# Attention decode with a gated feed-forward: wider runs for two weight matrices, keys three pairs ahead, a word-wise turn

## The chip, the cores and the metric

One core of a Trainium2 chip runs the whole kernel. The metric is the device time of one execution in microseconds (us); for the kernel before it is the median of three runs.

## The reference, cut to what matters

```
# B=8, D=512, Hq=32, Hkv=8, rep=4, Sk=4096, Dh=128, F=1792, all bfloat16
xn = layernorm(x)                                   # (8, 1, 512)
q  = (xn @ wq).reshape(8, 1, 32, 128)
W  = min(4096, max(256, Sk // 4))                   # 1024: only the last 1024 keys count
k, v = k_cache[:, :, Sk-W:], v_cache[:, :, Sk-W:]   # repeated for the 4 query heads of a key head
p  = softmax(q . k * Dh**-0.5)
s  = (p . v).reshape(8, 1, 4096) @ wo
g  = silu((gelu(xn @ w_gate) * (xn @ w_up)) @ w_down)
out = x + s * g                                     # (8, 1, 512)
```

One token of eight sequences. Each weight and each key and value of the window is used once for few rows, so some 47 MB are read for little arithmetic.

## The kernel before, in words

**Loads.** All large loads are issued by SyncE (SP) on one DMA queue, in program order, into a ring of nine buffers of 16 KB a partition (2 MB; pool `big`). A load waits until the work on the tile that had its buffer is done. The order is: `wq` in three DMAs (1, 1 and 2 MB), gate and up matrix, K0, K1, down matrix, V0, K2, V1, K3 and so on to K7, V6, V7, and then `wo`. K0 is the "key pair" of key head 0: one tile with the window of all eight sequences, 128 partitions by two *sets* by 32 keys of 128 elements. A partition holds 32 consecutive keys of one sequence, 8 KB in a run of memory. Set s = 2h + y has the four sequences of parity y. `load_pair` (L102) loads a pair in one DMA, or in two halves, one for each set; only V7 goes in halves. The list `pending` (L537) with `fetch` (L543) gives the order.

**Ahead of the keys.** Layer norm, the queries (L296, 32 matmuls, as `wq` lands), gate and up matmuls (L344), the queries transposed into `qT`, and the masks (`masks`, L239, on VectorE (DVE)).

**The main loop** (L560) runs over half steps t; s, i = divmod(t, 2). In step t a set s gets two of its four transposed quarters (`transpose_quarter`, L422): TensorE (PE) transposes four blocks of 128 x 128 words, two bfloat16 in one FP32 word (L425), and VectorE (L436) or ScalarE (ACT, L438) copies them out of PSUM to `kT`. One set behind follow the scores (L447, eight matmuls on four groups of 32 columns, the even and odd elements of the words), the mask with the row maximum (L455), and the maximum over each query's partitions (`maxima`, L466 and L471). Two sets behind follow the exponentials (L480, with the row sum), a copy of the row sum on GpSimd (POOL, L484), and `turn` (L490), which transposes 32 x 32 blocks of the probabilities. From step `LV` = 7 on, `value_half` (L496) multiplies with the values (L501, 16 matmuls a set in two halves). A value matmul takes a pair of keys at once, so its result has 2 x 128 columns of which one half belongs to each row; both go to `blk` (L508). `gather` (L512) sums each head's rows with eight FP32 matmuls (L518), which pick the right half, divides by the sum (L523, L525) and turns the result (L530) into `oR`, the left operand of the output projection. TensorE works in this written order: a matmul that waits for a load holds back all behind it.

**The feed-forward** hides in it: `hidden_steps` (L359), two in each step; `down` in steps 7 and 8, `fold` and `gate` in step 9.

**The end.** The output matrix comes in seven pieces; row 4p + r of each 512-row block of a head is at partition p, so the four rows of a partition are 4 KB in a run. Pieces are two of 1 MB (two heads each), three of 512 KB, and the last head as 384 and 128 KB. 128 matmuls (L605) sum them, two VectorE operations (L616, L617) apply gate and residual, and ScalarE issues the store (L618).

## Time and profile before

| | |
|---|---|
| median of 3 runs | 120.78 us (120.72 to 120.94) |
| the profiled execution, its own time | 120.92 us |
| its span | 119.1 us |
| granted TensorE clock, mean | 0.971 |
| PE busy | 83.4 us (70%), 974 matmuls |
| DVE / ACT / POOL busy | 64.2 / 56.2 / 5.5 us |
| DMA | 47.60 MB, 6557 packets, mean 400 GB/s |

The span is the profiled part of the execution, from its first to its last instruction; some 1.8 us of the execution lie outside it. Engine shares are averages over stages with different limits; a wait is worth what it moves at the end. "PEld" is TensorE's weight load. The chain that ended last is followed back from the last instruction, and names at each step what released it.

### The profile page before, as it was taken

Reading aid. Unit: us, or ns where it says so; the run is one execution under the profiler, and the core shown is the slowest. Engines: PE = TensorE matmul, PEld = TensorE weight load, DVE = VectorE, ACT = ScalarE, POOL = GpSimd, SP = SyncE. Lnnn points to the kernel's source line nnn. Section 1 sums busy time; section 2 is a strip of 40 time slices with the busy share of each in tenths; the row PEclk is TensorE's granted clock in tenths of the full one; section 3 lists DMA queues with packets and bytes.
Section 4 is the critical chain, followed back from the end, with each engine's and each line's share of the span. In section 5 each row is a group of like instructions: output and inputs, shape, how many; then the busy total and the mean of one; then the engine's idle time right before and its main releaser. Section 6 shows DMA issues by size and latency. Waiting matters only on the chain.

```text
span 119.1 us, 2381 instructions
## 1 busy us (share of the span) xinstructions
PE 83.4 (70%) x974; PEld 57.7 (48%) x974; DVE 64.2 (54%) x172; ACT 56.2 (47%) x94; POOL 5.5 (5%) x25
## 2 busy tenths in 40 slices
PE   0250629519956493979996898399999589966880
PEld 0110216119743353547764666356767348724660
DVE  1400131812799881848775577077787454854330
ACT  4100030204961881675795395249578634673200
POOL 7000000000000000000000000000000000000000
PEclk9999999999999999999999999769999976999999
DMA  3999999999999999999999999999999999999930
GB/s 96 424 451 435 425 424 415 432 421 432 437 420 418 435 424 435 421 416 435 421 432 418 435 424 421 427 427 427 424 440 416 424 429 427 424 409 421 414 136 3
DMA packets 6557, 47.60 MB, mean 400 GB/s; under 512 B 524, under 2 KB 660, under 8 KB 1684
## 3 DMA queue, kind: packets, MB, share of 16 engines
q1 hardware_dynamic: 6496, 47.45, 94.9%
q8 instruction: 7, 0.11, 0.3%
q10 hardware_dynamic: 52, 0.02, 0.1%
q14 instruction: 2, 0.02, 0.0%
HBM read 47.46 MB, written 0.01 MB: 399 GB/s over the span
## 4 chain that ended last, share of the span: by engine, by line
DMA 71%; PE 15%; ACT 5%; DVE 3%; SPq 2%; issue 1%; ACTq 0%
DMA big<-in_A_k_cache_dram 71%; PE kT_ps L425 7%; PE m_ps L518 2%; PE s L605 2%; PE o_ps L501 2%; ACT kT L438 2%; ACT p L480 1%; PE sc L447 1%; ACT L365 1%; SPq L145 1%; SPq L96 1%; PE m_ps L466 1%; DVE pT L490 1%; ACT blk L508 1%; ACT z L365 0%
## 5 line engine op out<-in xcount | busy, mean ns | idle before, releaser
L425 PE MATMUL kT_ps<-identf,big 128*128 128x128 f32 x256 | 39.7, 302 | 9.9 <-DMA big<-in_A_k_cache_dram 9.8
L438 ACT ACTIVATE kT<-kT_ps 128x1024 bf16<-128x1024 bf16 x32 | 32.5, 1021 | 28.7 <-PE kT_ps L425 28.5
L425 PEld LDWEIGHTS kT_ps<-identf,big 128*128 128x128 f32 x256 | 31.5, 154 | 18.2 <-DMA big<-in_A_k_cache_dram 9.9
L436 DVE COPY kT<-kT_ps 128x1024 bf16<-128x1024 bf16 x32 | 22.0, 688 | 19.5 <-PE kT_ps L425 19.3
L480 ACT ACTIVATE p<-sc_sb,bias 128x512 bf16<-128x512 f32 x16 | 11.5, 718 | 6.3 <-DVE bias L471 5.8
L501 PE MATMUL o_ps<-big,pT 128*32 128x256 bf16 x256 | 12.6, 283 | 0.5 <-ACT blk L508 0.5
L490 DVE STREAM_TRANSPOSE pT<-p 128x512 bf16<-128x512 bf16 x16 | 11.3, 705 | 2.3 <-ACT p L480 2.2
L466 PE MATMUL m_ps<-identf,top 128*128 128x128 f32 x32 | 7.4, 311 | 7.0 <-DVE top L455 5.6
L455 DVE CUSTOM_DVE_ANT_0 sc_sb<-sc,own 128x512 f32<-128x512 f32 x16 | 10.5, 659 | 0.7 <-PE sc L447 0.7
L447 PE MATMUL sc<-kT,zeros 128*32 128x512 bf16 x128 | 10.8, 415 | 0.1
L466 PEld LDWEIGHTS m_ps<-identf,top 128*128 128x128 f32 x32 | 4.9, 194 | 9.4 <-DVE top L455 6.7
L518 PE MATMUL m_ps<-blk,sums 128*128 128x129 f32 x64 | 9.0, 281 | 0.4 <-ACT blk L508 0.4
L501 PEld LDWEIGHTS <-pT 128*32 128x32 bf16 x256 | 5.5, 97 | 6.1 <-issue 1.8
L518 PEld LDWEIGHTS m_ps<-blk,sums 128*128 128x128 f32 x64 | 7.9, 191 | 1.0 <-ACT blk L508 0.6
L484 POOL COPY blk<-blk 128x1 f32<-128x1 f32 x16 | 2.9, 184 | 103.7 <-ACT p L480 99.4
L508 ACT ACTIVATE blk<-o_ps 128x256 f32<-128x256 f32 x16 | 6.1, 382 | 2.8 <-PE o_ps L501 2.8
L296 PE MATMUL sc<-big,zeros 128*32 128x512 bf16 x16 | 2.5, 610 | 6.1 <-DMA big<-in_A_wq_dram 6.1
L303 DVE CAST q_row<-sc 128x512 bf16<-128x512 f32 x2 | 1.3, 686 | 9.3 <-PE sc L296 9.3
L471 DVE CUSTOM_DVE_ANT_0 scr<-m_ps,same 128x128 f32<-128x128 f32 x16 | 4.6, 289 | 2.4 <-PE m_ps L466 2.4
L307 ACT ACTIVATE q_row<-o_ps 128x512 bf16<-128x512 f32 x2 | 1.1, 594 | 9.5 <-PE o_ps L296 9.5
L296 PEld LDWEIGHTS <-zeros 128*32 128x32 bf16 x32 | 1.2, 119 | 8.1 <-issue 7.6
L330 DVE COPY zeros<-kT_ps 64x128 bf16<-64x128 bf16 x4 | 1.1, 282 | 4.8 <-PE kT_ps L318 4.1
(68 smaller groups left out, 52.3 us busy)
## 6 DMA issues: line engine op xcount, KB each, us to landing
big<-in_A_k_cache_dram SPq DMA_DIRECT2D x8, 2048.0 KB, 32.2
big<-in_A_v_cache_dram SPq DMA_DIRECT2D x7, 2048.0 KB, 33.7
big<-in_A_wq_dram SPq DMA_DIRECT2D x2, 1024.0 KB, 5.8
big<-in_A_wq_dram SPq DMA_DIRECT2D x1, 2048.0 KB, 11.2
big<-in_A_v_cache_dram SPq DMA_DIRECT2D x2, 1024.0 KB, 30.0
big<-in_A_wo_dram SPq DMA_DIRECT2D x2, 1024.0 KB, 28.0
big<-in_B_w_gate_dram SPq DMA_DIRECT2D x1, 1792.0 KB, 15.0
big<-in_B_w_up_dram SPq DMA_DIRECT2D x1, 1792.0 KB, 18.6
```

The costliest lines, as they stand in the source:

```text
L425: nc.tensor.transpose(ps[:, c, :], K[s][:, 2 * (i * QP + c) : 2 * (i * QP + c) + 2, :] .rearrange("p c d -> p (c d)").bitcast(FP32), identf,)
L436: nc.vector.tensor_copy(out=out, in_=in_)
L438: nc.scalar.activation(out=out, in_=in_, func=ACT.Copy)
L447: nc.tensor.matmul(ps[32 * R : 32 * R + 32], qT[:, e, s].rearrange("p c b j -> p (c b j)"), t[:, :, 32 * R : 32 * R + 32, e], start=(e == ...
L455: nc.vector.tensor_tensor_reduce(out=sc[s], in0=ps.rearrange("p c k -> p (c k)"), in1=own.rearrange("p c b g -> p (c b g)"), op0=ALU.add, ...
L466: nc.tensor.matmul(ps, top.pop(s).to_broadcast([P, P]), identf, start=True, stop=True)
L471: nc.vector.tensor_tensor_reduce(out=scr, in0=ps, in1=same.rearrange("p x n -> p (x n)"), op0=ALU.add, op1=ALU.min, scale=-scale, scalar=- ...
L480: nc.scalar.activation(out=P_[s], in_=sc.pop(s), func=ACT.Exp, scale=scale, bias=biases.pop(s), accum_out=blk[s][:, 0, Dh : Dh + 1],)
L490: nc.vector.transpose(out=pT[s].rearrange("p c k -> p (c k)"), in_=P_.pop(s))
L501: nc.tensor.matmul(o_ps[s][32 * q : 32 * q + 32].rearrange("p c d -> p (c d)"), pT[s][:, c, :], V[s][:, 2 * c : 2 * c + 2, :].rearrange("p ...
L508: nc.scalar.activation(out=blk[s][:, :, 0:Dh], in_=o_ps.pop(s), func=ACT.Copy)
L518: nc.tensor.matmul(ps, sums[:, c, b].rearrange("p j b f -> p (j b f)"), t[:, c, :], start=(b == 0 and c == 0), stop=(b == NB - 1 and c == 1),)
```

## The change

- `wo` is read with eight rows (8 KB) a partition, over blocks of two heads: `oR` and `gather` work on pairs of heads (`x = h % 2` goes to partitions 0 to 63 or 64 to 127 of one PSUM tile). Pieces are three of 1 MB, then 512, 384 and 128 KB.
- The two halves of a value result are joined ahead of the gather: ScalarE scales one by `half[:, 0]`, VectorE adds the other times `half[:, 1]`. `blk` has 129 columns in place of 258, a head has four gather matmuls with 64 output rows in place of eight with 128, and the copy of the row sum is gone.
- The first two k-rows of `wq` come in one DMA of 2 MB (16 KB a partition).
- Keys come three pairs ahead of the values in place of two. K0 and K7 come in halves. Values start at step 9, `down` runs in steps 8 and 9, `fold` and `gate` in step 10; `gather` runs one step later.
- `turn` transposes words of two probabilities. So the score columns are put in the order (pair of chunks, key, which of two), in the score matmul's operand and the mask, and a value matmul's weights have a step of two.
- Masks but for the reductions, two small copies and one memset go from VectorE to GpSimd, one copy to ScalarE.

```diff
-    m_top, m_out = m_ps[:, 0:P], m_ps[:, P : P + Dh + 1]
+    m_top = m_ps[:, 0:P]
+    m_out = m_ps[:, P : P + 2 * (Dh + 1)].rearrange("p (a d) -> p a d", a=2)
...
-    HB = 2 * SET // (rep * D)
+    R8 = 2 * rep
...
     def load_wo(h, r0, n, nh=1):
...
+        t = wo_at(h)[:, h % 2 : h % 2 + nh, r0 * D : (r0 + n) * D]
+        src = A_wo.rearrange("(h p k) n -> p h (k n)", p=P, k=R8)
+        src = src[:, h : h + nh, r0 * D : (r0 + n) * D]
+        if nh == 1:
+            nc.sync.dma_start(out=t[:, 0, :], in_=src[:, 0, :])
...
-    for k0, cuts in ((0, (1, 1)), (2, (2,))):
+    for k0, cuts in ((0, (2,)), (2, (2,))):
...
-        nc.vector.tensor_copy(out=xf, in_=ps)
+        nc.scalar.activation(out=xf, in_=ps, func=ACT.Copy)
...
-    own = consts.tile([P, CP, 32 // G, G], FP32, name="own")
+    own = consts.tile([P, CP // 2, 32 // G, G, 2], FP32, name="own")
...
-    sums = consts.tile([P, 2, 2, rep, B, PB], FP32, name="sums")
+    sums = consts.tile([P, NB, 2, rep // 2, B, PB], FP32, name="sums")
...
-    oR = rows.tile([P, Hkv, rep, 32], BF16, name="oR")
+    oR = rows.tile([P, Hkv // 2, 2 * rep, 32], BF16, name="oR")
...
-                    t[:, :, 32 * R : 32 * R + 32, e],
+                    t.rearrange("p (c a) k e -> p c k a e", a=2)[
+                        :, :, 32 * R : 32 * R + 32, :, e
+                    ],
...
-        nc.gpsimd.tensor_copy(
-            out=blk[s][:, 1, Dh : Dh + 1], in_=blk[s][:, 0, Dh : Dh + 1]
-        )
...
     def turn(s):
-        pT[s] = p_pool.tile([P, CP, 32], BF16, name="pT", bufs=3)
+        pT[s] = p_pool.tile([P, CP // 2, 32, 2], BF16, name="pT", bufs=5)
         nc.vector.transpose(
-            out=pT[s].rearrange("p c k -> p (c k)"), in_=P_.pop(s)
+            out=pT[s].rearrange("p c k a -> p (c k a)").bitcast(FP32),
+            in_=P_.pop(s).bitcast(FP32),
         )
...
-                pT[s][:, c, :],
+                pT[s][:, c // 2, :, c % 2],
...
-            nc.scalar.activation(out=blk[s][:, :, 0:Dh], in_=o_ps.pop(s), func=ACT.Copy)
+            ps, o = o_ps.pop(s), blk[s][:, 0:Dh]
+            nc.scalar.activation(
+                out=o, in_=ps[:, 0, :], func=ACT.Copy, scale=half[:, 0:1]
+            )
+            nc.vector.scalar_tensor_tensor(
+                out=o, in0=ps[:, 1, :], scalar=half[:, 1:2], in1=o,
+                op0=ALU.mult, op1=ALU.add,
+            )
...
     def gather(h):
+        x = h % 2
+        t = [blk.pop(h * NB + b) for b in range(NB)]
+        for hh in range(2):
+            for b in range(NB):
+                nc.tensor.matmul(
+                    m_out[64 * x : 64 * x + 64, hh, :],
+                    sums[:, b, hh].rearrange("p j b f -> p (j b f)"), t[b],
+                    start=(b == 0), stop=(b == NB - 1), skip_group_check=True,
+                )
+        if x == 0:
+            return
...
+        nc.vector.tensor_tensor(
+            out=o.rearrange("p r a i -> p a i r"),
+            in0=ps[:, :, 0:Dh].rearrange("p a (i r) -> p a i r", r=R8),
+            in1=rec.unsqueeze(2).unsqueeze(3).to_broadcast([P, 2, Dh // R8, R8]),
+            op=ALU.mult,
+        )
...
-    pending = [("K", 0), ("K", 1), ("D", 0)]
+    AHEAD = 3
+    pending = [("K", h) for h in range(AHEAD)] + [("D", 0)]
     for h in range(Hkv):
         pending.append(("V", h))
-        if h + 2 < Hkv:
-            pending.append(("K", h + 2))
+        if h + AHEAD < Hkv:
+            pending.append(("K", h + AHEAD))
...
-                    2 if (k, i) == ("V", Hkv - 1) else 1,
+                    2 if (k, i) in (("K", 0), ("K", Hkv - 1), ("V", Hkv - 1)) else 1,
...
-    LV = 7
+    LV = 4 * AHEAD - 3
...
-        if i == 1 and s >= 5 and s % 2 == 1:
-            gather((s - 5) // 2)
+        if i == 1 and s >= 6 and s % 2 == 0:
+            gather((s - 6) // 2)
...
+        if t == LV - 1:
+            fetch("D", 0)
+            down(0)
+        if t == LV:
+            down(1)
+        if t == LV + 1:
+            fold()
+            gate()
...
-    pieces = [(0, 0, rep, 2), (2, 0, rep, 2)]
-    pieces += [(h, 0, rep, 1) for h in range(4, Hkv - 1)]
-
-    pieces += [(Hkv - 1, 0, rep - 1, 1), (Hkv - 1, rep - 1, 1, 1)]
+    pieces = [(0, 0, R8, 1), (1, 0, R8, 1), (2, 0, R8, 1)]
+    pieces += [(3, 0, 4, 1), (3, 4, R8 - 5, 1), (3, R8 - 1, 1, 1)]
```

## The prediction

> **What bounds the kernel now.** I read the slices of the page first, then the DMA queues, then the chain that ended last, and at last the end of the span with windows and the issue groups.
>
> ```profile
> DMA  3999999999999999999999999999999999999930
> GB/s 96 424 451 435 425 424 415 432 421 432 437 420 418 435 424 435 421 416 435 421 432 418 435 424 421 427 427 427 424 440 416 424 429 427 424 409 421 414 136 3
> ...
> q1 hardware_dynamic: 6496, 47.45, 94.9%
> q8 instruction: 7, 0.11, 0.3%
> ```
>
> The DMA engines are full from the second slice to the 38th. 47.45 MB go through one queue at 409 to 451 GB/s, with no gap, and the kernel has to read all of them. So the span is the stream, plus what stands ahead of it (some 1.8 us) and what follows its last byte.
>
> The chain that ended last seems to say something else: from 95.7 us on it names nearly only TensorE.
>
> ```profile
> 95.72 1.13 PE kT_ps L425 x8
> ...
> 113.43 1.68 PE s L605 x112
> 115.11 0.04 issue
> 115.14 0.60 PE s L605 x16
> ```
>
> The 128 last matmuls (L605, the output projection) look like a PE tail. Two other answers show that it keeps step with the DMA. The first is the issue groups (line 128, and the last output piece), the second windows of 1 us; in these the columns from the third are PE, PEld, DVE, ACT and POOL busy (with counts), granted clock, DMA share, GB/s.
>
> ```profile
> L128 SPq DMA_DIRECT2D big<-in_A_wo_dram x7: 327/2092/7705, 80.0 to 103.0; - x7
> ...
> big<-in_A_wo_dram SPq DMA_DIRECT2D x1, 128.0 KB, 12.4
> ```
>
> ```profile
> 113.00:114.00 1.00, 1.00 (x52) 0.88 (x54) 0.49 (x2) 0.00 (x0) 0.00 (x0) 1.00 0.80 303
> 114.00:115.00 1.00, 1.00 (x80) 0.98 (x69) 0.34 (x2) 0.00 (x0) 0.00 (x0) 1.00 0.34 130
> 115.00:116.00 1.00, 0.69 (x24) 0.30 (x15) 0.23 (x1) 0.00 (x0) 0.00 (x0) 1.00 0.01 3
> ```
>
> The last piece is issued at 103.0 and lands 12.4 us later, at 115.4. Four matmuls use it, and PE ends at 115.74: 112 matmuls took 1.68 us (15 ns each), the last 16 took 0.60. The end is set by the last byte, with TensorE some tenths behind it at most: it is a tie, and relief of TensorE alone brings next to nothing. The windows also show that the 16 engines do not end together: at a share of 0.80, 0.34 and 0.01, the mean engine ends near 114.1, the slowest after 115.
>
> **The change part by part.** The profiled execution took 120.92 us (span 119.1 and 1.8 around it), the median of the runs is 120.78; I work out a difference and take it from the median.
>
> *Output matrix in runs of eight rows.* Bytes stay, packets grow: six of the eight heads went in 4 KB runs and now go in 8 KB runs (three pieces of 1 MB, 3.15 MB); the last two heads stay at 4, 3 and 1 KB. Two windows of 6 us compare the sizes, 107 to 113 us (output matrix, 4 KB) and 60 to 66 us (keys and values, 8 KB):
>
> ```profile
> DMA packets 694, 2.52 MB, mean 420 GB/s; under 512 B 64, under 2 KB 64, under 8 KB 694
> ...
> DMA packets 332, 2.57 MB, mean 429 GB/s; under 512 B 19, under 2 KB 19, under 8 KB 19
> ```
>
> 3.15 MB at 420 GB/s are 7.49 us, at 429 they are 7.33: 0.16 us less. The windows of the page bound it: if 426 (40 to 96 us) against 415 (104 to 113 us) is taken, 0.20; if nothing of it is the packet, 0. I take 0.16. By the Trainium skill (DMA: Bandwidth & Descriptors, Why small descriptors are slow) a packet costs about 3 bus cycles beside one for each 32 bytes; worked out from it as an estimate, two 4 KB packets take 262 cycles and one of 8 KB 259, and the gain would be 0.09 us. The trace shows a difference of 2.1%, not 1.2%.
>
> *Query matrix in 16 KB runs.* 2.1 MB go from two DMAs with 8 KB runs to one. The matmuls of L296 start with each landing: 5.58, 8.01 and 12.88 us. So 1 MB in 8 KB runs took 2.43 us and 2 MB in 16 KB runs 4.87: no difference. The rate from 6 to 12 us (441 against 426) would give 0.17. I take 0.05, near the landings.
>
> *Keys three pairs ahead, first and last key pair in halves.* SP issues K2 ahead of the down matrix, and so each K one V earlier; bytes and number of DMAs (30) are the same. The last K lands one pair (2.1 MB, 4.9 us) earlier than 95.7, the value pair V5 takes its place, and V6, V7 and the output matrix land as before, V7 at 95.7 + 9.85 = 105.6. No gap comes into the stream if each buffer is free in time: a pair is issued some 32 us ahead of its landing, six pairs of 4.9 us. The new order holds K2 until V0 has landed (its second half is transposed behind the first value matmuls, since TensorE goes in order), about 47 us (K0 at 26.3, then 3.9 pairs of 4.9 us up to V0 make 45.4, and the transposes); what reuses its buffer, K6, lands near 80, so some five pairs remain queued. Cost: nothing; without that cover each gap would cost its length.
>
> *The word turn, joined halves, fewer gather matmuls.* L518 goes from 64 to 32 matmuls (8 for each head took 1.06 us; some 4 us of PE in all). L490 (705 ns for 512 words of 2 bytes) turns 256 words of 4; from L530 (128 wide, 312 ns) and L490 the slope is 1.0 ns an element, so 0.44 us, or 0.7 if it goes by bytes. Added: the copy of L508 falls from 256 to 128 columns, and a DVE addition on 128 columns follows it (L616, 292 ns). POOL gets the masks (2 us on DVE near 23 us, a time with nothing to do until K0). All that lies under the stream: in the window from 40 to 96 us PE is busy for 46.67 of 56 us (83%), DVE for 36.80.
>
> The new score matmuls read keys in alternating order, and the weights of L501 come with a step of two words. No row shows either: L447 reads at a step of two elements in 415 ns. Between no cost and twice (8 for a set in 0.62 us, 16 sets) it is up to 1.2 us a pair; the idle of PE, 17% of 9.8, is 1.7. I take nothing, as L447 already reads with a step.
>
> *What is late next.* After V7 (105.6): 16 value matmuls 0.62, copy 0.39, addition 0.3, 4 gather matmuls 0.71, reciprocal 0.17, the division on 256 elements (0.7 as two of L525; 1.24 by L372, which writes with a like scatter: 2175 ns for 448), turn 0.5. That ends near 109.7; the last byte comes at about 115.2. The tie becomes a slack of over 5 us, and the last byte alone decides.
>
> *The price of idling.* With that slack, TensorE stands nearly idle from 109 on. The trace shows what follows: it waited from 74.3 to 76.2 and from 94.1 to 95.7 for keys, and then
>
> ```profile
> 77.00:78.00 1.00, 1.00 (x6) 0.78 (x4) 0.64 (x2) 0.00 (x0) 0.00 (x0) 0.50 1.02 434
> ```
>
> half the clock for 3.4 us. The last matmuls will run so. L296 (610 ns at the start, not yet warm) against L447 (415), both 512 columns: 49 ns for 128 columns, weight load 119 against 97, and the other three at double spacing: about 0.1 us for the last four. Bounds: 0, and 0.25 if the 12 before them queue up too. I take 0.1; it comes at the very end, nothing hides it.
>
> Sum: -0.16 - 0.05 + 0.10 = -0.11 us; with the tie gone (up to 0.15 in runs where TensorE is the later one; I take 0.07) -0.18: 120.60 us. About 0.2%, or 0.24 us, is what a measurement of this kernel can tell from no change, so the sum lies just inside.
>
> **Rivals.** *A, the cold array takes it all:* 0.25 at the end against 0.2 from the packets: 120.75. For it speaks the clock row above; against it, that only 16 matmuls stand behind the last pieces. The Trainium skill (TensorE: Matmul & The Clock Gate, Part 1) has the rule: an idle window of about 3.4 us halves the clock. The trace agrees, 3.4 us at 0.50.
>
> *B, slower: an instruction fetch on an engine already late.* The seven packets of q8 are 16 KB each (0.11 MB), 0.3% of 16 times 119.1 us, some 0.8 us each. Whatever engine carries one is late by that, and the packet behind it stretched; this is how the slowest engine comes to end over 1 us after the fastest. TensorE runs 2 x 974 instructions; 64 go away. The seventh fetch comes among the L605 matmuls, now at 113.8 us when half of the engines are done; in the changed kernel those matmuls follow the pieces, so it is asked for at about 111 to 113, with the stream running. On an engine not yet late it changes nothing; on one that is, the end moves by 0.8 us up to the whole spread seen at the end, some 1.4: 121.4 to 122.0. Against it: so far no engine seems to have had two, as the ends differ by one such delay.
>
> *C, the full gain:* packets 0.20 and 0.17, the array warm, the tie 0.1: -0.47, 120.3.
>
> *D, TensorE or DVE gets the bound* (alternating reads, scattered writes): it decides from a loss of 5 us in the tail or 1.7 a pair, far above the prices here: 2.0 a pair would be 0.3 over the idle time, 2.4 in eight pairs: 123.0.
>
> **How the numbers follow.** Forecast 0.55 (120.35 to 120.75: 0.24 faster, 0.31 same), A 0.14 (same), C 0.16 (faster), B 0.12 and D 0.03 (slower). Faster by over 0.2% 0.40, within 0.45, slower 0.15. The range reaches from 120.2, just under C, to 121.1: B's and D's ends stay out.
>
> **What would show it.** After: the wo stretch at 425 GB/s or more where it was 415 to 420; the last key wait near 91 instead of 95.7; L605 spread over 108 to 115 with gaps released by the DMA, clock 0.50 at the end; PE's last matmul 0.3 to 0.5 us behind the last landing. It is wrong if the DMA share falls below 1 anywhere ahead of 113, if L605 ends without waiting for the last piece, or if one engine ends over 1.5 us after the others.

## The result, and the profile after

The changed kernel takes 125.34 us (median of six runs, 124.67 to 125.57), the kernel before 120.87 beside it: a ratio of 1.0359, interval 1.0338 to 1.0379. It is 3.6% slower, and the forecast of 120.6 us with its range up to 121.1 is wrong. Several of the kernels below, and the kernel before, have two groups of run times some 2 us apart; ratios compare the lower group, while medians and ranges are of all runs, and where a profiled run is of the upper group its own time is given.

The profiled execution took 124.67 us, its span is 122.9 us. From the page: busy time of TensorE, granted clock, rate of the DMA in 40 slices of 3.07 us.

```profile
PE 92.4 (75%) x974; PEld 55.8 (45%) x974; DVE 64.8 (53%) x165; ACT 56.2 (46%) x95; POOL 4.4 (4%) x19
...
PEclk9999999955899999999999999999999999855999
...
GB/s 109 416 427 435 434 439 405 427 421 427 429 453 404 428 429 424 429 427 424 429 424 424 427 427 421 429 427 427 427 421 427 427 427 421 427 427 392 69 5 3
```

The stream of bytes does what was forecast: it is over in the 38th slice, near 115 us, as before. But TensorE's last matmul now ends at 119.6 us in place of 115.7, and the clock falls to 0.8 in slice 35 and to half in slices 36 and 37. TensorE is busy for 92.4 us in place of 83.4, with the same 974 matmul records. The groups of instructions say where (the last two columns ahead of the second bar are us in all and ns of one; behind it stands the idle time of the engine just before them):

```profile
L444 PE MATMUL sc<-kT,zeros 128*32 128x512 bf16 x128 | 20.1, 704 | 0.6 <-ACT kT L435 0.6
...
L523 PE MATMUL m_ps<-blk,sums 128*64 128x129 f32 x64 | 11.0, 304 | 1.2 <-DVE blk L510 1.2
L465 PE MATMUL m_ps<-identf,top 128*128 128x128 f32 x32 | 7.0, 303 | 4.9 <-DVE o L535 3.5
...
L486 DVE STREAM_TRANSPOSE pT<-p 128x256 f32<-128x256 f32 x16 | 7.1, 442 | 2.8 <-ACT p L479 2.8
...
L535 DVE TENSOR_TENSOR o<-m_ps,rec 128x256 bf16<-128x256 f32 x4 | 5.1, 1282 | 0.1
```

Three things to see: the score matmuls (L444) went from 415 to 704 ns; the division (L535) takes 1282 ns; and TensorE waits for that division (3.5 us, ahead of the maxima L465). The chain that ended last, in order of time (start, length), from the last score matmuls to the last output matmuls:

```profile
101.81 1.28 PE sc L444 x8
...
104.13 0.89 PE m_ps L523 x6
105.25 1.28 DVE o L535
106.58 0.81 PE m_ps L465 x2
...
109.38 1.07 PE o_ps L498 x13
110.47 0.38 ACT blk L507
110.87 0.36 DVE blk L510
111.28 1.55 PE m_ps L523 x6
112.83 0.82 PE o_ps L498 x16
113.68 0.38 ACT blk L507
114.08 0.36 DVE blk L510
114.48 0.65 PE o_ps L498 x16
115.15 0.38 ACT blk L507
115.55 0.36 DVE blk L510
115.96 0.89 PE m_ps L523 x6
117.08 1.33 DVE o L535
118.43 0.46 DVE oR L542
118.93 0.66 PE s L618 x32
```

No DMA is in this part of it; the last matmul that waits for a load at all is one at 46.72 us. One set of value matmuls follows the other through one PSUM buffer: matmuls, copy, addition, then the next set or the gather. The division stands in this chain twice. Windows of the kernel before and of the changed one (columns from the third: PE, PEld, DVE, ACT and POOL busy with counts, granted clock, DMA share, GB/s), a stretch of the middle and one of the output matrix; before first:

```profile
50.00:90.00 40.00, 34.85 (x391) 24.98 (x391) 26.61 (x73) 26.39 (x44) 1.47 (x8) 0.96 1.01 426
104.00:113.00 9.00, 6.42 (x94) 4.29 (x93) 4.27 (x14) 4.08 (x9) 0.37 (x2) 1.00 1.02 415
```

```profile
50.00:90.00 40.00, 38.03 (x380) 22.97 (x376) 26.68 (x72) 24.88 (x41) 0.00 (x0) 1.00 1.01 426
104.00:113.00 9.00, 6.03 (x56) 3.85 (x60) 3.29 (x9) 1.44 (x4) 0.00 (x0) 0.64 1.01 423
```

In the middle TensorE is now busy for 38.03 of 40 us (95%, was 87%). In the other stretch the rate rose from 415 to 423 GB/s and the clock fell to 0.64.

### The profile page after: what moved, and what is told of

Its sections match the earlier page's. It is cut to its first block, busy times and chain, and to the rows that moved or that the text cites. A ratio compares the mean times of both kernels' runs of the same rounds, so it can differ in the third digit from the quotient of the medians.

```text
span 122.9 us, 2366 instructions
## 1 busy us (share of the span) xinstructions
PE 92.4 (75%) x974; PEld 55.8 (45%) x974; DVE 64.8 (53%) x165; ACT 56.2 (46%) x95; POOL 4.4 (4%) x19
## 4 chain that ended last, share of the span: by engine, by line
PE 47%; DMA 37%; DVE 8%; ACT 4%; issue 1%; SPq 0%; ACTq 0%
DMA big<-in_A_v_cache_dram 27%; PE kT_ps L422 18%; PE sc L444 11%; DMA big<-in_A_wq_dram 10%; PE m_ps L523 7%; PE o_ps L498 7%; DVE o L535 4%; PE m_ps L465 3%; ACT kT L435 2%; DVE blk L510 1%; ACT blk L507 1%; ACT p L479 1%; DVE rec L532 1%; DVE sc_sb L454 1%; PE s L618 1%
## 5 line engine op out<-in xcount | busy, mean ns | idle before, releaser
L422 PE MATMUL kT_ps<-identf,big 128*128 128x128 f32 x256 | 37.9, 292 | 2.6 <-DMA big<-in_A_k_cache_dram 2.6
L422 PEld LDWEIGHTS kT_ps<-identf,big 128*128 128x128 f32 x256 | 29.3, 147 | 12.7 <-issue 5.9
L444 PE MATMUL sc<-kT,zeros 128*32 128x512 bf16 x128 | 20.1, 704 | 0.6 <-ACT kT L435 0.6
L498 PEld LDWEIGHTS <-pT 128*32 128x32 bf16 x256 | 6.2, 102 | 15.4 <-issue 13.6
L523 PE MATMUL m_ps<-blk,sums 128*64 128x129 f32 x64 | 11.0, 304 | 1.2 <-DVE blk L510 1.2
L465 PE MATMUL m_ps<-identf,top 128*128 128x128 f32 x32 | 7.0, 303 | 4.9 <-DVE o L535 3.5
L507 ACT ACTIVATE blk<-o_ps,half 128x128 f32<-128x128 f32 x16 | 5.9, 366 | 9.8 <-PE o_ps L498 9.8
L523 PEld LDWEIGHTS m_ps<-blk,sums 128*64 128x64 f32 x64 | 7.2, 146 | 4.6 <-DVE blk L510 2.6
L486 DVE STREAM_TRANSPOSE pT<-p 128x256 f32<-128x256 f32 x16 | 7.1, 442 | 2.8 <-ACT p L479 2.8
L510 DVE SCALAR_TENSOR_TENSOR blk<-o_ps,half,blk 128x128 f32<-128x128 f32 x16 | 5.6, 348 | 5.5 <-ACT blk L507 5.5
L465 PEld LDWEIGHTS m_ps<-identf,top 128*128 128x128 f32 x32 | 5.0, 197 | 5.9 <-DVE o L535 4.2
L535 DVE TENSOR_TENSOR o<-m_ps,rec 128x256 bf16<-128x256 f32 x4 | 5.1, 1282 | 0.1
```

Of the source, the lines that this page charges most:

```text
L422: nc.tensor.transpose(ps[:, c, :], K[s][:, 2 * (i * QP + c) : 2 * (i * QP + c) + 2, :] .rearrange("p c d -> p (c d)").bitcast(FP32), identf,)
L444: nc.tensor.matmul(ps[32 * R : 32 * R + 32], qT[:, e, s].rearrange("p c b j -> p (c b j)"), t.rearrange("p (c a) k e -> p c k a e", a=2)[: ...
L465: nc.tensor.matmul(ps, top.pop(s).to_broadcast([P, P]), identf, start=True, stop=True)
L486: nc.vector.transpose(out=pT[s].rearrange("p c k a -> p (c k a)").bitcast(FP32), in_=P_.pop(s).bitcast(FP32),)
L498: nc.tensor.matmul(o_ps[s][32 * q : 32 * q + 32].rearrange("p c d -> p (c d)"), pT[s][:, c // 2, :, c % 2], V[s][:, 2 * c : 2 * c + 2, :]. ...
L507: nc.scalar.activation(out=o, in_=ps[:, 0, :], func=ACT.Copy, scale=half[:, 0:1])
```

## The experiments

The theory formed from this: the tail behind the last scores is a serial chain, and the change made it longer at several places (slow score reads ahead of it, the scattered division in it, an addition for each set, half a clock while it waits), until it passed the end of the stream. Rivals: one edit alone is the cause, the stream itself suffers, or the new order of the loads does.

### One part alone, in the kernel before

**b_ahead3: keys three pairs ahead.**

```diff
-    pending = [("K", 0), ("K", 1), ("D", 0)]
+    AHEAD = 3
+    pending = [("K", h) for h in range(AHEAD)] + [("D", 0)]
...
-    LV = 7
+    LV = 4 * AHEAD - 3
...
-        if i == 1 and s >= 5 and s % 2 == 1:
-            gather((s - 5) // 2)
+        if i == 1 and s >= 6 and s % 2 == 0:
+            gather((s - 6) // 2)
```

> The kernel before with keys three pairs ahead alone (values from step 9, gather and down matmuls moved as in after, two more buffers for the turned probabilities). Theory 4: one value set more stands behind the last keys and V5, not K7, is the load that the rest waits for, but without the added link and with the short division the chain has room: 120.8 to 122.5 us. If the three pairs ahead are the whole cause: 124 us.

Measured: 120.89 us, ratio 0.9987 (0.9962 to 1.0013): no difference. Its timeline of TensorE (start, us, instructions, in brackets the idle time before and what ended it):

```profile
100.40 0.63 PE L447 MATMUL sc<-kT,zeros 128*32 128x512 bf16 x8 [0.53 <-ACT kT L438]
...
103.10 0.49 PE L466 MATMUL m_ps<-identf,top 128*128 128x128 f32 x2 [0.65 <-DVE o L525]
...
111.23 1.30 PE L607 MATMUL s<-big,oR 128*32 128x128 bf16 x80
113.36 0.41 PE L607 MATMUL s<-big,oR 128*32 128x128 bf16 x16 [0.83 <-DMA big<-in_A_wo_dram]
114.61 0.41 PE L607 MATMUL s<-big,oR 128*32 128x128 bf16 x16 [0.84 <-DMA big<-in_A_wo_dram]
115.56 0.64 PE L607 MATMUL s<-big,oR 128*32 128x128 bf16 x16 [0.55 <-DMA big<-in_A_wo_dram]
```

This is the picture that the prediction had drawn for the whole change: the output matmuls start at 111.23 and wait three times for the DMA. So the new order of the loads costs nothing and does make slack, some 3 us (the 128 matmuls take 1.97 us where nothing holds them, as in b_div, so they could have ended at 113.2 in place of 116.2). And it brings nothing, since the last byte stays where it was.

**b_turn: the word turn** (with the alternating score reads and the mask's order that it asks for).

```diff
-                    t[:, :, 32 * R : 32 * R + 32, e],
+                    t.rearrange("p (c a) k e -> p c k a e", a=2)[
+                        :, :, 32 * R : 32 * R + 32, :, e
+                    ],
...
-            out=pT[s].rearrange("p c k -> p (c k)"), in_=P_.pop(s)
+            out=pT[s].rearrange("p c k a -> p (c k a)").bitcast(FP32),
+            in_=P_.pop(s).bitcast(FP32),
```

> The kernel before with the word turn alone added. Theory 1: L447 goes from 415 to about 704 ns, PE is busy for 92 us, and the time goes to 124 to 127 us, as TensorE was in a tie with the stream and gets 9 us more, of which some 3.5 fit into its waits. Theories 2 and 3: TensorE has idle time enough, 120.5 to 121.5 us.

Measured: 120.69 us, 0.9981 (0.9958 to 1.0003). The score matmul has the price of the changed kernel, and the kernel before absorbs it: TensorE is busy for 89.7 us (76%), and its last output matmuls still wait for the DMA.

```profile
L448 PE MATMUL sc<-kT,zeros 128*32 128x512 bf16 x128 | 20.1, 704 | 0.1
...
114.81 0.57 PE L609 MATMUL s<-big,oR 128*32 128x128 bf16 x16 [0.52 <-DMA big<-in_A_wo_dram]
```

From 50 to 90 us TensorE is busy for 38.12 of 40 us here, as much as in the changed kernel (38.03). So a middle at 95% is not by itself what makes the kernel late.

**b_join: halves joined ahead of the gather** (two gather matmuls a head).

```diff
-            nc.scalar.activation(out=blk[s][:, :, 0:Dh], in_=o_ps.pop(s), func=ACT.Copy)
+            nc.scalar.activation(
+                out=o, in_=ps[:, 0, :], func=ACT.Copy, scale=half[:, 0:1]
+            )
+            nc.vector.scalar_tensor_tensor(
+                out=o, in0=ps[:, 1, :], scalar=half[:, 1:2], in1=o,
+                op0=ALU.mult, op1=ALU.add,
+            )
```

> The kernel before with the halves of the value results joined ahead of the gather alone (copy on ScalarE, then addition on VectorE; two gather matmuls a head in place of four). Theory 4: each of the last three value sets gets a link of 0.4 us in series, and the last gather is 0.5 us shorter: 121 to 122 us. If the join is no part of the cause: 120.3 to 120.8.

Measured: 122.73 us (121.73 to 122.97, four runs), ratio 1.011 (1.0046 to 1.0175): slower although TensorE has 32 records fewer (942 against 974). The profiled run is its fastest; the tail of its timeline:

```profile
108.95 0.49 PE L519 MATMUL m_ps<-blk,sums 128*128 128x129 f32 x2 [1.31 <-DVE blk L507]
109.37 0.62 PE L496 MATMUL o_ps<-big,pT 128*32 128x256 bf16 x16
110.85 0.96 PE L496 MATMUL o_ps<-big,pT 128*32 128x256 bf16 x16 [0.86 <-DVE blk L507]
```

The next set waits 0.86 us for copy and addition; with the copy alone it waited 0.49 (the row of 111.61 in the kernel before, shown further down). One edit of the change is thus by itself a loss, in the tail.

**b_runs: 8 KB runs for the output matrix, the query matrix in one DMA fewer.** It leaves out the matching order of `oR`, so the rows of the output matrix meet other weights; the traffic is the change's.

```diff
-    for k0, cuts in ((0, (1, 1)), (2, (2,))):
+    for k0, cuts in ((0, (2,)), (2, (2,))):
...
-    pieces = [(0, 0, rep, 2), (2, 0, rep, 2)]
-    pieces += [(h, 0, rep, 1) for h in range(4, Hkv - 1)]
+    pieces = [(0, 0, rep, 2), (2, 0, rep, 2), (4, 0, rep, 2), (6, 0, rep, 1)]
```

> The kernel before with the loads of the output matrix in runs of 8 KB (pieces as in after) and the first half of the query matrix in one load; matmuls as before, so the rows of the output matrix meet the wrong weights, which is the part that is changed. Prediction: the last piece lands 0.2 us earlier, and 0.1 to 0.3 us are gained, 120.5 to 120.7. If wider runs bring nothing: 120.8.

Measured: 121.01 us, 1.0032 (1.0006 to 1.0058). From 104 to 113 us the rate is 422 GB/s where it was 415, as forecast. The time does not show it; if anything it is 0.3% longer. Why the 0.1 to 0.2 us that the rate should give are missing is open.

**b_div: the division's scattered write alone.**

```diff
-            out=o, in0=ps[:, 0:Dh].rearrange("p (i r) -> p r i", r=rep),
+            out=o.rearrange("p r i -> p i r"),
+            in0=ps[:, 0:Dh].rearrange("p (i r) -> p i r", r=rep),
```

> The kernel before with the scattered write in its division alone (eight divisions on 128 elements; by L372 and L535 some 0.65 us each in place of 0.35). If a scattered write is harmful wherever it stands: its 0.3 us come twice in the chain at the end and may lower the clock, 121.3 to 123 us. If it takes the long chain of the changed kernel as well: 120.7 to 121.0.

Measured: 121.81 us (120.65 to 123.59), 1.004 (1.0009 to 1.0071).

```profile
L525 DVE TENSOR_SCALAR o<-m_ps,rec 128x128 bf16<-128x128 f32 x8 | 6.2, 777 | 0.3
```

777 ns against 351 for the same 128 elements with the step on the reading side (that row of the kernel before). Two of the eight divisions stand near the end. The ratio is small, but the median of all ten runs is 1.0 us above that of the kernel before beside it (120.81), four of them took 122.95 to 123.59, and in the profiled run (121.31 us) the clock from 104 to 113 us is 0.63, where the kernel before had 1.00. So the scattered write is not free even here.

### One part undone, in the changed kernel

**a_div: the division writes in order and reads with the step.**

```diff
-            out=o.rearrange("p r a i -> p a i r"),
-            in0=ps[:, :, 0:Dh].rearrange("p a (i r) -> p a i r", r=R8),
-            in1=rec.unsqueeze(2).unsqueeze(3).to_broadcast([P, 2, Dh // R8, R8]),
+            out=o,
+            in0=ps[:, :, 0:Dh].rearrange("p a (i r) -> p r a i", r=R8),
+            in1=rec.unsqueeze(1).unsqueeze(3).to_broadcast([P, R8, 2, Dh // R8]),
```

> The kernel after with the division alone changed back to an ordered write (PSUM read with a step); the slow score reads stay. If the scattered division is the largest single cause (2.5 us between a_psum and a_psumdiv): 122 to 123 us. If it counts only once the score matmuls are short again, as TensorE is then waiting for other engines: under 1 us, 124.5 or more.

Measured: 120.78 us (120.50 to 123.98), 0.9992 (0.9972 to 1.0011). Six of ten runs took 120.80 us or less, the others 122.36 or more; the profiled one took 123.98, so its trace shows durations, not where the others gain. Its timeline, the division and the maxima behind it:

```profile
104.36 0.42 DVE L535 TENSOR_TENSOR o<-m_ps,rec 128x256 bf16<-128x256 f32 x1
```

```profile
104.84 0.49 PE L465 MATMUL m_ps<-identf,top 128*128 128x128 f32 x2 [0.72 <-DVE o L535]
```

0.42 us in place of 1.28, and TensorE waits 0.72 in place of 1.57. This edit of three lines takes the whole loss away by the median, with the score matmuls still at 704 ns. Two divisions shorter by 0.86 us each are 1.7 us of the 4.5; where the rest comes from in the faster runs, no trace shows. Their granted clock is 0.97 to 0.99, that of the four others 0.94 to 0.97.

**a_psum: chunk pairs put side by side by the key transposes' write into PSUM**, so that the score matmuls read one run.

```diff
-                ps[:, c, :],
+                ps[:, c // 2, :, c % 2],
...
-                    t.rearrange("p (c a) k e -> p c k a e", a=2)[
-                        :, :, 32 * R : 32 * R + 32, :, e
-                    ],
+                    t[:, :, 64 * R : 64 * R + 64, e],
```

> The kernel after, with the word turn kept, but the key transposes write the two chunks of a pair interleaved into PSUM (a step of two words in the output of L422), so that the copies and the score matmuls read in one run with the old step of two elements. Theory 1: L444 back at 415 ns; if the stepped PSUM write costs nothing (L422 stays at 292 ns), 120.2 to 120.8 us; if it doubles L422, worse than after, 130 or more. Theories 2 and 3: 124 us or more.

Measured: 123.88 us, 1.0259 (1.0197 to 1.0321).

```profile
L422 PE MATMUL kT_ps<-identf,big 128*128 128x128 f32 x256 | 38.3, 295 | 4.3 <-DMA big<-in_A_k_cache_dram 4.3
...
L444 PE MATMUL sc<-kT,zeros 128*32 128x512 bf16 x128 | 10.6, 408 | 0.6 <-ACT kT L435 0.6
```

The same order of the columns at 408 ns, and the transposes that now write at a step (L422) pay nothing: 295 against 292 ns. 9.5 us of score matmuls are gone, and the time falls by 1.5: its last scores start at 100.06 in place of 101.81, and the rest of the tail remains.

**a_noturn: the word turn undone** (halfword turn, keys in their old order).

```diff
-            out=pT[s].rearrange("p c k a -> p (c k a)").bitcast(FP32),
-            in_=P_.pop(s).bitcast(FP32),
+            out=pT[s].rearrange("p c k -> p (c k)"), in_=P_.pop(s)
```

> The kernel after with the word turn alone undone (probabilities turned as bfloat16, score columns and masks in the old order); all else as after. Theory 1 (the score matmuls read keys alternately from two chunks and so take 704 ns in place of 415; 16 sets at 0.56 us more make TensorE the bound): L444 back at about 415 ns, PE busy down by some 9 us to 83, the last matmuls wait for the last output piece again, 120.3 to 120.8 us. Theory 2 (three keys ahead puts the values 5 us later, and TensorE never catches up): still 124 us or more. Theory 3 (the division with scattered writes, 1282 ns in place of 2 x 351, holds back matmuls that share its PSUM tile): 123.5 to 125.

Measured: 124.34 us, 1.0288 (1.0242 to 1.0334). Score matmuls at 399 ns, and 1.0 us gained where a_psum gained 1.5 (the longer turn may account for the rest; that was not measured by itself).

**a_ahead2: keys two ahead again**, values from step 7, the gather a step earlier.

```diff
-    AHEAD = 3
+    AHEAD = 2
...
-    LV = 4 * AHEAD - 3
+    LV = 7
```

> The kernel after with keys two pairs ahead, values from step 7 and the gather one step earlier, as before; the rest as after, the word turn too. Theory 1: the score matmuls still take 704 ns and TensorE still has more work than the stream takes, but its values begin one pair (4.9 us) earlier: 123 to 126 us. Theory 2: back to about 120.8 us.

Measured: 125.13 us, 1.0358 (1.0313 to 1.0402): taking this part back wins nothing. The way there is another, though. Its last scores start at 107.84 us in place of 101.81, but fewer sets follow them and the clock is 1.00 from 104 to 113 us in place of 0.64. So a loss of this size does not need the half clock; in the changed kernel the longer tail, in part at half clock, eats up the 6 us that the earlier keys had won.

### Two parts undone

**a_psumdiv** is a_psum and a_div together.

```diff
-                ps[:, c, :],
+                ps[:, c // 2, :, c % 2],
...
-            out=o.rearrange("p r a i -> p a i r"),
+            out=o,
```

> The kernel a_psum (after, with key chunks interleaved in PSUM, 123.9 us) with the division of the gather writing in order and reading PSUM with a step, as before, in place of the scattered write. Theory 4 (the end is a serial chain behind the last keys, and the division stands in it twice, once ahead of the last maximum and once ahead of the last output matmuls): L533 goes from 1.28 to about 0.6 us, and the time falls by twice the difference, 1.3 us, to 122.6. Rival theory 5 (the end is late because the middle is late: TensorE falls behind there): under 0.3 us, as the middle has DMA waits.

Measured: 121.44 us (120.67 to 122.77), 1.0013 (0.9966 to 1.0061). **a_psumdivnojoin** takes in addition the joined halves back (eight gather matmuls a head, one copy, no addition), **a_psumdiv_o2** keeps them and gives the value matmuls a second PSUM buffer:

```diff
-    ps_kT = ctx.enter_context(tc.tile_pool(name="ps_kT", bufs=4, space=PSUM))
+    ps_kT = ctx.enter_context(tc.tile_pool(name="ps_kT", bufs=3, space=PSUM))
...
-    ps_o = ctx.enter_context(tc.tile_pool(name="ps_o", bufs=1, space=PSUM))
+    ps_o = ctx.enter_context(tc.tile_pool(name="ps_o", bufs=2, space=PSUM))
```

The edit of the former is:

```diff
-            nc.scalar.activation(
-                out=o, in_=ps[:, 0, :], func=ACT.Copy, scale=half[:, 0:1]
-            )
-            nc.vector.scalar_tensor_tensor(
-                out=o, in0=ps[:, 1, :], scalar=half[:, 1:2], in1=o,
-                op0=ALU.mult, op1=ALU.add,
-            )
+            nc.scalar.activation(out=blk[s][:, :, 0:Dh], in_=o_ps.pop(s), func=ACT.Copy)
```

> The kernel a_psumdiv (121.4 us) with the halves of a value result not joined: one copy of 256 columns as before, and eight gather matmuls a head on half the rows (four more than joined, some 0.5 us of TensorE a head). Theory 4 (the link copy, then addition, in front of the next set's matmuls is the rest of the loss): the gaps of 0.8 us ahead of each value set behind the last keys go, TensorE stays busier and its clock up, 120.4 to 121.0 us. If the join is harmless here: 121.4 or more, by the added matmuls.

> The kernel a_psumdiv with two PSUM buffers for value results (three in place of four for the key transposes), so that the next set's value matmuls need not wait for copy and addition. If the price of the join is the single buffer: 120.4 to 120.9 us. If it is the longer way from a set's matmuls to its gather: no change, 121 to 122.5; the lost transpose buffer may cost some tenths in the middle, which has waits to hide it.

Measured: 120.70 us, 0.9986 (0.9964 to 1.0008), ten runs within 120.66 to 120.86; and 120.86 us, 1.0001 (0.9984 to 1.0018), within 120.75 to 121.02. Either way the runs, which spread over 2.1 us in a_psumdiv, lie close together. In both traces the last output matmuls are released by the DMA (in the first with waits of 0.57 and 0.50 us). No version went below that: nothing here beats the kernel before by more than the measurement can tell.

**a_divnojoin** is a_div with the halves not joined, but with the slow score reads.

```diff
-                nc.tensor.matmul(
-                    m_out[64 * x : 64 * x + 64, hh, :],
-                    sums[:, b, hh].rearrange("p j b f -> p (j b f)"), t[b],
...
+                for c in range(2):
+                    nc.tensor.matmul(
+                        m_out[64 * x : 64 * x + 64, hh, :],
+                        sums[:, b, hh, c].rearrange("p j b f -> p (j b f)"),
+                        t[b][:, c, :], start=(b == 0 and c == 0),
```

> The kernel a_div (ordered division, slow score reads kept) with the halves not joined (one copy, eight gather matmuls a head on half the rows). If the join's link makes the chain at the end long enough for the clock to fall in some runs: all runs in one group at 120.4 to 120.8 us. If the split in two groups has another cause: both groups stay.

Measured: 123.48 us (its profiled run 125.17), 1.0243 (1.0171 to 1.0316), while the same edit was harmless behind a_psumdiv. TensorE is busy for 99.2 us (80% of the span; 93.4 in a_div), 39.73 of the 40 us from 50 to 90, and its last scores start at 104.02 us against 100.92: 3.1 us late. With slow reads, the eight gather matmuls make TensorE the bound of the middle. So the parts do not add up; each is hidden or not by what the others leave.

### What the waiting costs

**a_psumorder** is a_psum with the gather written behind the maxima, so that a maximum does not wait for a division. The same two lines move down in their step.

```diff
-        if i == 1 and s >= 6 and s % 2 == 0:
-            gather((s - 6) // 2)
...
+        if i == 1 and s >= 6 and s % 2 == 0:
+            gather((s - 6) // 2)
```

> The kernel a_psum with the gather written behind the maximum in its step in place of ahead of it. Theory 4: the last maximum (L463 at 104.5 us in a_psum, held 1.6 us by the division and 2 us by the gather ahead of it) comes near 101, and the whole chain behind it some 2.5 to 3.5 us earlier: 120.8 to 121.5 us. Theory 5: no change, 123.9.

Measured: 123.18 us, spread over 121.22 to 123.91; the ratio 1.0073 (1.0013 to 1.0133) rests on few of its runs. Against a_psum (123.88) it points to a gain and no more, less than was expected.

**a_sep: the gather's result in a PSUM tile of its own**, to the same end.

```diff
-    m_out = m_ps[:, P : P + 2 * (Dh + 1)].rearrange("p (a d) -> p a d", a=2)
+    m_outs = {}
...
+        if h == 0:
+            m_outs[0] = ps_s.tile([P, 2, Dh + 1], FP32, name="s")
+        m_out = m_outs[0]
```

> The kernel after with the gather's result in a PSUM tile of its own (the feed-forward's, free by then; the output sum goes to the tile of the maxima), so that a maximum need not wait for the division. If the division costs by holding TensorE through the shared tile: the waits of L465 for it (7.8 us in all) go, the last maximum comes some 1.5 us earlier, 121 to 123.5 us. If it costs by keeping VectorE from its other work: 124.5 to 125.5.

Measured: 123.65 us, 1.0224 (1.0154 to 1.0294): 1.7 us of the 4.5. The last maxima come at 103.77 in place of 106.58 us, and then the next value set waits 2.90 us: the addition (L510) that it needs comes behind the slow division on VectorE.

**a_warm: five sets of eight matmuls that nobody reads**, behind the last keys, to hold the clock.

```diff
+    def idle_work():
+        ps = ps_kT.tile([P, QP, P], FP32, name="kT_ps")
+        for c in range(2 * QP):
+            nc.tensor.transpose(ps[:, c % QP, :], identf, identf)
...
+            if s == 16:
+                idle_work()
...
+            if s >= NS and i3 == 1 and s3 < NS - 1:
+                idle_work()
```

> The kernel after with five times eight matmuls more that nothing reads (transposes of the identity into a free PSUM buffer), in the steps behind the last keys where TensorE waits for copy, addition or division. Theory 6 (half of the loss is the clock, which falls to 0.50 at the end because TensorE waits there): granted clock 1.00 to the end, and in spite of the added work 122 to 123.5 us. If the clock is a side show: 125.3 or more, by up to the 5 us of added matmuls.

Measured: 123.73 us, 1.0236 (1.0198 to 1.0274). Granted clock on its page, and the end of its timeline:

```profile
PEclk9999999999999999999999999999999999999998
```

```profile
115.83 1.52 PE L628 MATMUL s<-big,oR 128*32 128x128 bf16 x96
117.98 0.63 PE L628 MATMUL s<-big,oR 128*32 128x128 bf16 x32 [0.63 <-DVE oR L548]
```

Added work makes the kernel 1.6 us faster: the clock stays up, a value set takes 0.62 us in place of 1.04, and the gather behind it 1.09 us, where two records and six had taken 0.69 and 1.55. The division still releases the last matmuls.

**a_warmdiv: both**, the unread matmuls and the ordered division.

```diff
-            out=o.rearrange("p r a i -> p a i r"),
+            out=o,
...
+                idle_work()
```

> The changed kernel with the division written in order and with the five sets of eight unread matmuls behind the last keys. Theory (the scattered division costs 0.86 us twice in the serial tail, and the waiting there lets the clock fall to half, some 2 us more): with both taken away TensorE reaches the output matmuls before the last byte, the clock stays at 1.0, the last output matmuls wait for the DMA, and all times lie together at 120.5 to 121.2; no second group above 122. Rival (the gain of the ordered division comes from something else, and the two groups of times seen with it have nothing to do with the clock): two groups again, 120.7 and 122.4 to 124. Rival (the unread matmuls themselves cost): 121.5 to 122.5 in one group, with the output matmuls released by TensorE.

Measured: 121.70 us (121.00 to 122.26, 12 runs), 1.0047 (1.0019 to 1.0076). By the median that is the third branch of what was expected, and TensorE is indeed the later one at the end: the 128 output matmuls start at 114.06 without a wait and end at 116.03. But that is only 0.3 us behind the 115.74 of the kernel before, and the spans of all twelve runs lie at 119.1 to 119.6 us, close to the 118.7 to 119.0 of a_div's six faster runs. What is longer is the part outside the span, 1.75 to 2.75 us where the other kernels have 1.7 to 1.9; why is open. The spans near 122 us that a_div has are gone. That they come from the clock is thus made likely, not shown.

**a_o2: only the second buffer for the value matmuls**, the division left scattered, with the edit of the pools shown above.

```diff
-    ps_o = ctx.enter_context(tc.tile_pool(name="ps_o", bufs=1, space=PSUM))
+    ps_o = ctx.enter_context(tc.tile_pool(name="ps_o", bufs=2, space=PSUM))
```

> The changed kernel with two buffers for the value matmuls' PSUM (three instead of four for the turned keys), the scattered division left in. Theory (four sets of value matmuls stand in one serial chain behind the last keys, each waiting for the copy and the addition of the set before; the division stands in that chain twice): the sets of two run together, some 0.9 us each time, 2 us in all, the division still at 1.28 us: 122.5 to 123.8. Rival (only the division counts, whatever the chain around it): 125.0 to 125.5, as the change. Rival (the serial sets are the whole of it): 120.7 to 121.

Measured: 121.47 us (120.72 to 122.99, 12 runs), 1.0045 (1.0008 to 1.0081), more than the theory had allowed. Its timeline (of the slowest run, 122.99 us):

```profile
106.41 0.49 PE L465 MATMUL m_ps<-identf,top 128*128 128x128 f32 x2 [1.56 <-DVE o L535]
106.83 1.06 PE L498 MATMUL o_ps<-big,pT 128*32 128x256 bf16 x32
108.91 1.98 PE L523 MATMUL m_ps<-blk,sums 128*64 128x129 f32 x8 [1.02 <-DVE blk L510]
110.83 1.90 PE L498 MATMUL o_ps<-big,pT 128*32 128x256 bf16 x32
```

Two sets now run together. So the division is not the only lever: the single buffer is another, and by the median either of the two takes away nearly the whole loss (125.34 us down to 120.78 and 121.47). The rival that the scattered division alone is the cause falls.

## Why the prediction was wrong

**The step that failed is "What is late next".** It started a chain at V7's landing (105.6 us) and counted one set of 16 value matmuls, one copy, one addition, four gather matmuls and a division, to end near 109.7 with "a slack of over 5 us". In the trace nothing waits for V7. The last maxima run at 106.58 us, and behind them the chain of waits still holds three sets of value matmuls (109.38, 112.83, 114.48), each with copy and addition through one buffer, two gathers and a division. The output matmuls start at 116.76, not 109.7. Part of that is the list itself and not the price of its terms: in b_ahead3, with the new order of loads and the old prices, they start at 111.23, 1.5 us behind the forecast. (The terms as listed add up to 109.0 or, with the dearer division, 109.5.) The kernel before had the same sets in its tail, so this could have been read there:

```profile
107.78 0.49 PE L466 MATMUL m_ps<-identf,top 128*128 128x128 f32 x2 [1.41 <-DVE top L455]
108.20 0.62 PE L501 MATMUL o_ps<-big,pT 128*32 128x256 bf16 x16
...
110.50 0.62 PE L501 MATMUL o_ps<-big,pT 128*32 128x256 bf16 x16
111.61 0.62 PE L501 MATMUL o_ps<-big,pT 128*32 128x256 bf16 x16 [0.49 <-ACT blk L508]
112.16 1.27 PE L518 MATMUL m_ps<-blk,sums 128*128 128x129 f32 x8
113.36 2.36 PE L605 MATMUL s<-big,oR 128*32 128x128 bf16 x128
```

The table sets the tail of the changed kernel against that of b_ahead3, which has the new order of loads and none of the rest. Both profiled executions have half a clock in part of their tails; starts and lengths in us:

| stretch | changed | b_ahead3 | longer by |
|---|---|---|---|
| start of the last scores | 101.81 | 100.40 | 1.41 |
| from there to the last maxima | 4.77 | 2.70 | 2.07 |
| from there to the first output matmul | 10.18 | 8.13 | 2.05 |
| the output matmuls, without waits for the DMA | 2.80 | 1.97 | 0.83 |
| sum | | | 6.36 |

The slack was some 3 us (113.2 against 116.2), so 3.4 us remain, and the two spans differ by 122.9 - 119.5 = 3.4 us. That the two agree is bookkeeping, as both are taken from the same two traces; and these are the fastest run of the changed kernel and the slowest of b_ahead3, so that the table explains 3.4 of the 4.5 us between the medians. What the rows consist of is read from the traces: slow reads and the divisions ahead (first row; the last scores start at 100.06 in a_psum and at 100.92 in a_div), the division at 1.28 against 0.35 and eight scores at 1.25 against 0.63 (1.55 of the second), in the third four sets of values, the first of them right behind the maxima, that each take some 0.4 us longer to the next (the addition takes 0.35) and the maxima, which run at half the clock, and the division once more (fourth: the last 32 output matmuls wait 0.64 us for it and its turn). It also shows why two fixes are worth no more than one: what is gained below the stream's end cannot be seen.

The steps, in their order:

- *The stream bounds, TensorE ties:* right for the kernel before, and for the changed one no longer true.
- *Runs of 8 KB:* the rate nearly right (423 GB/s, "425 GB/s or more where it was 415 to 420"), the time not: b_runs shows no gain, so no run shows the 0.16 and 0.05 us of the sum.
- *Keys three ahead at no cost:* right by the time (b_ahead3 and a_ahead2), and b_ahead3 waits for keys for the last time at 91.18 us, as forecast.
- *The word turn:* 0.44 us forecast, 442 ns measured. "L518 goes from 64 to 32 matmuls" was wrong: L523 has 64 records, as L518 had. A head had four gather matmuls before the change too; each shows as two records (b_join, with two a head, has 32), and records had been taken for matmuls.
- *Alternating reads, "I take nothing":* wrong. The bound given, twice, 1.2 us a pair, is what came (8 matmuls 1.25 us in place of 0.62). The value was taken from a row with a step of two elements, which is not the nearest: the new operand goes back and forth between two chunks 512 bytes apart. That 1.2 fits into the 1.7 of idle time was right for b_turn. In the changed kernel it did not fit beside the waits for the division: no matmul waits for a load behind 46.72 us. With either of the two undone TensorE is on time again, and waits for a load near 96 us (0.59 us in a_psum, 0.22 in a_div).
- *The division, 0.7 to 1.24:* right, 1.28, by the row of the like scatter (L372). It was laid under a slack that was not there, and its second place, ahead of the last maxima, was not looked at.
- *The price of idling, 0.1 us:* that waits halve the clock was right, the place and the size were not. The half clock met the serial tail, not the last four matmuls, and holding it up is worth 1.6 us (a_warm). The 610 ns of L296, taken for a cold array, come with a granted clock of 1.00 in the trace, so that price is not shown. And the 3.4 us at half clock that rival A points to stand behind a wait of 1.96 us; an idle window of 3.4 us this trace does not show.
- *Rivals:* A, B and C need the last byte to decide and did not come about; that a fetch of instructions makes one DMA engine late, as B has it, no view here shows. D, slower because TensorE or VectorE gets the bound through "alternating reads, scattered writes", is nearest to what happened, at 0.03, though not through them alone. Its threshold, a loss of 5 us in the tail, rested on the same slack; the loss was 6.4 and the slack 3. The sign "if L605 ends without waiting for the last piece" is what the trace shows: those matmuls (L618 now) wait for the division.

The Trainium skill has a rule that would have warned: SBUF — State Buffer, Door 1: The DMA port swizzle, says that an access pays when it crosses to a new 16-byte line without having used the one before at least twice. The trace agrees on both operands: keys 512 bytes apart, read in turn, 704 against 415 ns; two-byte elements written 64 bytes apart, 1282 against 420 ns; a step of two elements, four on a line, has the lower price, 399 to 415 ns. The same note warns that PSUM accesses that are not contiguous slow matmuls down significantly; the trace does not agree for a_psum, whose transposes write every second word of PSUM at 295 against 292 ns.

## What to carry to other kernels

Before calling a stage hidden, list everything that is still to run when its last input lands, in the program's order and with the buffers it shares, and set the sum against the end of the stream; the slack is what is left, and what is added to that tail beyond the slack is paid in full. Where a layout must change, look for the side on which the step is cheap (here a read of PSUM by VectorE, 0.42 us, and a write to PSUM by TensorE, 3 ns) and not on scattered writes or on a moving operand that jumps with each element. Test parts alone and undone: here the word turn, the earlier keys and the longer runs cost next to nothing alone, the joined halves and the scattered division 1.9 and 1.0 us by the median, and all together 4.5.

## What the runs showed of the hardware

- Scattered two-byte writes of VectorE cost 5.0 ns an element (1282 for 256), or 6.1 (777 for 128); the same elements written in order, with the step on the read of PSUM, 1.6 (0.42 us) and 2.7 (351 ns). Each is the whole instruction divided by its elements.
- A moving operand that alternates between two places 512 bytes apart takes 704 ns for 512 columns, against 399 to 415 at a step of two elements. The same columns ordered by a stepped write to PSUM cost 3 ns.
- Work that nobody reads made a kernel faster (125.34 to 123.73 us), since it kept the granted clock at 0.996 in place of 0.944. The Trainium skill (TensorE: Matmul & The Clock Gate, HAM oscillation — how this bites in real kernels) describes waits of over 3.4 us that halve the clock. Here single waits of 0.2 to 1.6 us, one after the other, were enough: from 106 to 113 us the clock is 0.53 with TensorE recorded as busy for 5.16 of 7 us. In a_ahead2 single waits of up to 1.1 us in the tail left it at 1.00, so where the line lies is open.
